# A new table of stage offsets for the planner that orders a fused attention and MLP kernel

## The chip, the core and the metric

The kernel runs on one core of a Trainium2 chip. The time is that of one execution on the device, in microseconds; of several runs the median is told. TensorE is called PE here, VectorE DVE, ScalarE ACT, GpSimd POOL and SyncE SP, as the profile has them.

## The reference

Local attention with block summaries, then a normalised MLP with a residual. Four batches, eight heads, 768 positions, head size 64; the model width is 512, the hidden width 2048. `v_sum` is the mean of v over blocks of 32, `k_sum` the maximum of k.

```python
scores_l = scale * np.matmul(q, k.transpose(0, 1, 3, 2))
mask_l = np.abs(pos[:, None] - pos[None, :]) < 16
scores_s = scale * np.einsum('bhsd,bhnd->bhsn', q, k_sum) + np.log(32)
scores_all = np.concatenate([np.where(mask_l, scores_l, -1e9), scores_s], axis=-1)
a = softmax(scores_all)
x = concat_heads(np.matmul(a, np.concatenate([v, v_sum], axis=2)))
xn = (x - mean(x)) / np.sqrt(var(x) + 1e-6) * g_ln
out = x + np.maximum(xn @ w_ch1, 0.0) @ w_ch2
```

## The kernel before

The rows of the 24 tiles of 128 positions (T, six to a batch) go through attention in 48 halves of four heads (t = 2T and 2T + 1). For one half, PE computes the scores `s` (`qk`, or `early_qk` for the first twelve halves, which are those of the first batch), DVE adds the mask and takes the maximum, ACT takes the exponential (`softmax`), the probabilities `p` are transposed to `pT`, and PE multiplies them with v into `o` (`pv`, `early_pv`). For the first batch the transposing is done on PE (tile `pp`) with a copy on ACT; later it is a transposing DMA that SP issues.

`ln(T)` normalises the 128 rows and writes them as two float16 halves, `x16`; `lnT(T)` has SP issue a DMA that transposes x16 into `xt`. One `xt` holds two tiles T, so that xt_2 takes x16_4 and x16_5. The MLP goes over twelve groups g of two tiles and eight steps j each. `g1(s)`, with s = 8g + j, makes the hidden tile `h` from xt and the first weights (24 matmuls; h16 to h23 are those of g = 2); ACT and DVE take it out of PSUM as two float16 parts. `g2(s)` adds its product with the second weights to the two accumulators `a` (`a0` those of g = 0); after j = 7 DVE adds the residual and SP stores. The very last accumulator of half a width is called `last`.

Weights arrive as pairs of 32-bit words (`raw`, 512 KB each). `merge_w` puts each of the 16 + 16 blocks together in three DVE steps (`m1_f`, `m2_f`), `gram` multiplies each block with itself on PE to bound its size, `scale_w1` and `scale_w2` make scales of that, and `split_w` splits each block into two float16 parts (`w_u` and `w`; the order's names for the latter are `w2_0` to `w2_15`), the first part on ACT, the second on DVE. `scale_w2` needs all 16 blocks of `gram` for the second weights, and every `a` needs `scale_w2`. For each batch after the first, maxima of k (`kmax`), sums of v (`vsum`) and bounds are taken from loads of `ks`, `vs` and `qa` that go through the buffers `bst` and `qs`; `batch_vput` has SP write vsum into the tiles of v with eight small DMAs.

No engine's order is written out. Every call is recorded as an operation of a stage, a call of a `step` function with its arguments. `issue` ranks each operation by the longest chain behind it, adds 16 times its stage's entry of the table `ORDER` (935 numbers), plans the program forward with `schedule`, where each engine takes its ready operation of the lowest rank, and then in turn backward and forward, `ROUNDS` times; of the forward plans the one with the earliest end is kept, and the operations are issued in the order of its planned starts:

```python
rank, best = [r + early[x.stage] for r, x in zip(rank, self.ops)], None
for _ in range(ROUNDS):
    start, end = self.schedule(rank, after, False)
    if best is None or max(end) < best[0]:
        best = (max(end), start, end)
    rank = [-x for x in self.schedule([-x for x in end], then, True)[1]]
```

On the chip each engine works through its own instructions strictly in that order, and SP issues all DMAs in its order. All recorded instructions carry the line that issues them, L333, so they are told apart by their tiles.

Of the kernel before, what the change touches and what calls it, by code (L numbers as in the profile page):

```python
# [49 lines left out]
PVS = 4  # L50

ORDER = (
    "Z{Yv`E;RrEJtzPGqUitsIN$&OEZ_hC@BaV)CiMUR_T~ToEd2lfG~@sOdfWg10~r7Sd;tIevEKjxD(L_J-sb=R?(_fuR@VRjF8Kfdfdl{m5aa*<"
# [4 lines left out]
    "7r&Mp7|%nkqm1y=w7$Ljz8L)!oUG3x*So(li~q4)p)Arb%pAUFU3HShobw(tM{ITHW?8}R@CPWJ!*B<TPD!pHyrlO6y7lI#EfSs4HT7cKw*w*&"
    "wHohSeRoCg2^au@&riz)yBHwgd$wlM$z2>1X0ef$6a(zpNrwG;pVeeeJO(f<Gc)(8Lq&>#Q+iopN>mgoQfFw+13?h60_G5-JmZyNvr-"
    "2wmre;@z=%mM%axD)^YN#y_k(iQ*!uq6NhOaK4>DF6Tel;r>aul@i3jQaoo84&;gFd+Z{nh*d0R~G;Pi~axqbqoLiMFs!>;`aal2=f2`@z($UD"  # L60
    "&+tF^9ld}{nY>eBnJQhJpBLv8x;Tm|NH;{Soi<`jPU>eN7VoSECT=lqy_*0KnVZ<{3`$eR4@Pl6Y~H6D&YVBRr3G;{KEhL0{s8~GbsQ7#UB6wT"
    "LJ(8&h`KQ_1*vf|Lgz%uNVLT<^TWydG`PRq0s;TsRsZ66x;v*(hUFr;Q#;t1IqvZ$OHfYzWM+E_4NP$j{pDwydD4my8ZwE&mI5(h6Dfr8Z7_-"
    "RNVjnYT*C>{uKZKrN;mNUIPFC4(0#<_SygcR}cUIa~S{t^!xw+l@b5|MPUE{Y3Tp|1Ni^{6aWAKgb@G$L#O}$U=jcTfG7X}&;0-Y>-"
    "Ycv!xjJl^eO-V?HvFB$pHWW^veJLfE)k-=I;OhDGdMs#Q*>RJ1GDFiBJFld?o+@#w7p%pfUge5+DEo%sv1BV>kc+N-"
    "Y2YKNA1|vl9RSE&u=k2LAv5Y&ZY_(kcJ|JU0LU2nGNEkKX_PWi<c*Tgw0c!^i*s^Z5V&@#z2mE9n3K<NyEvyHEfCRv7>Qhy?%u$PNGi8Z-"
    "a^=N13}=lTEt*a-jtPVoQ#1^NH~C>H<#p%nlCf*Sw;k~aVV3OE1&Yc>D?K_&nI#7zJIMic-"
    "5s2BhMZTbKIwg3PBG!g&+r49f93@iWufBpaeRuljLWG(;zN96ziJpcdzwe0`@x7h#x04M+eBme*ZP5uA>Vdnq;!w~=gwg3PCECB!j3jhEA+1vm"
    "Bch~>_9Q^<PO7Z{y91s8i5a|E^_b31WHvj+tD98W*5dZ)G#vK3v*9HIpr6m9WnEwC&#r^;PTM_^OOYi^x{Pq9;KOX=9VFLgFu=)T0ryKwPF!cZ"
    "bH_HG2UhDt=pBVrECdvQ*nacnFjPU>efyn>=h`Im&x(NUPw738NUakNCkQ4v_iv0ioaoqp^blU&_Y61WNZ!!P?;lcm^(dGaDy7&M8%o6|rd;tI"
    "e#k~Lj5y1cdgWmuDKG*;M$Ke0}@B#n;8r}c@5#9g)N!|bdInMw8lq~=NK?(o>_`d)DEE)g+M+X1^?cM+XQ``UluO9#aYOeqP&9VRg;Q{~vL+Jn"  # L70
    "il;!{be)RwU6|MjO{~7=Qhp_+u=Mew^V7LGOPU!#tx!wQ&e)|9a7>@t{BG~``dei^^bff?O#ialLtTF%q@74eRLgfGd3lsnVtQ`OVBo+Vw#1sG"
    "kR__1*W!C@y8Uz3UIRF3u-rfKI%E<r!kG22*r1}5<BP0L-"
    "h{XT@M%e%Va^C;{qV@m(Ow#}VbJqX=koo`r3*rC&GWq}i)Ykw1efa<Xq~QPmmJ9#@9mN0t9k2iYZr1<*{>1<PD3$;Jz~=w|yZQhBquu}iC@la0"
    "?8X28<=g-NgV+E60{#F0G!Fm(rP2TYM&|$jpbY>3;{gBwp11%1Llgi2BoY7sIqd)c9m@azOfUcd*DC-3MgIT)V-"
    "ElT+YbN$%N76tcoF~ryW;=<1Qq}QDG&evpBMlD1n&R;#K8amz{CIlK=c3qh6MlsG|&J4PaXgOIR*d#;wb<Cj1vF=W~%@H^Wp#hj`IKi6|(>T{o"
    "DWlHSz!dpY;F#P~HFkAQ}JwG6ettef$6an)v_!D&7D8k>UUUiu3>f$pioZiN^o`z!CrerMdtA-q!#Bi{=0Sin9Ozfa3rEw)g-47ux^-"
    "AoKtKCIA2b&C&n=^z{G#O8@`>e;)t<G~WOJeFp#l5CH%HXUqTp`U3y}!mR)Qj4=QJcm@CfLDc{Ma_;~CH~|0v4)Xv1jOYLVx6c3n^&0>HlnVd="
# [1038 lines left out]
```

## Time and profile before

| what | before |
| --- | --- |
| median of 3 runs | 643.07 us (639.03, 643.07, 643.48) |
| the profiled execution | 637.87 us |
| its span | 635.9 us |
| PE busy | 623.9 us (98%) |
| DVE busy | 440.5 us (69%) |
| ACT busy | 379.3 us (60%) |
| POOL busy | 198.8 us (31%) |
| DMA queue of the kernel | 93.34 MB, 56.8% of 16 engines' span |
| granted TensorE clock | 1.00 |

The span runs from the first instruction to the last; the profiled execution's own time has 1.97 us more around it. The end of a matmul is modelled, so a busy PE can still be waiting a little between two matmuls. In the time line a row gives the start, the time taken, the engine, what is written from what, how many, and in brackets how long the engine had been idle and what ended that. An SPq row is SP issuing a DMA, not the transfer. Buffer numbers are left out in the profile, so that h16 and h17 are both `h`.

### The profile page before, as it was taken

To read this page: it belongs to the slowest core of one execution; us is meant where nothing else is said; L and a number is where in the kernel's file an instruction comes from. 1 tells how busy PE (TensorE), PEld (TensorE's weight loads), DVE (VectorE), ACT (ScalarE), POOL (GpSimd) and SP (SyncE) were. 2 spreads that over 40 slices of the span, in tenths; PEclk is the share of its full clock that TensorE was granted. 3 is DMA by queue.
4 is the path that set the end of the run, shared out by engine and by line. 5 is a ranking of instruction groups with operands and counts; after the bars stand their busy time and mean duration, and the time that the engine had idled before them with its cause. 6 is when DMAs were issued, how large, how long until landed. Compare 5 with 4: busy or idle time off the path is not lost.

```text
span 635.9 us, 13651 instructions
## 1 busy us (share of the span) xinstructions
PE 623.9 (98%) x4795; PEld 442.5 (70%) x4795; DVE 440.5 (69%) x1158; ACT 379.3 (60%) x986; POOL 198.8 (31%) x406
## 2 busy tenths in 40 slices
...
GB/s 303 247 193 281 260 296 214 128 134 101 160 204 134 110 149 160 175 158 159 198 170 162 168 136 123 121 107 163 111 129 129 155 145 95 61 84 51 18 1 33
DMA packets 134837, 94.19 MB, mean 148 GB/s; under 512 B 88561, under 2 KB 119281, under 8 KB 134770
## 3 DMA queue, kind: packets, MB, share of 16 engines
q1 hardware_dynamic: 134770, 93.34, 56.8%
q8 instruction: 37, 0.61, 0.4%
q14 instruction: 30, 0.25, 0.1%
...
## 4 chain that ended last, share of the span: by engine, by line
PE 76%; DVE 10%; DMA 9%; ACT 3%; issue 1%; POOL 1%; SPq 0%; ACTq 0%; DVEq 0%; POOLq 0%
PE a L333 35%; PE h L333 31%; DVE m L333 4%; PE o L333 4%; PE s L333 4%; DMA raw<-in_w 3%; DMA spare_x<-in_qe 2%; DMA spare_x<-in_va 2%; DVE x L333 1%; DVE h_x L333 1%; DMA pT<-p 1%; ACT p L333 1%; DMA qs<-in_ks 1%; PE last L333 1%; DVE vsum L333 1%
## 5 line engine op out<-in xcount | busy, mean ns | idle before, releaser
L333 PE MATMUL h<-xt,w_u 128*128 128x256 f16 x2304 | 267.3, 273 | 4.3 <-issue 2.1
L333 PEld LDWEIGHTS <-w_u 128*128 128x128 f16 x2304 | 224.2, 98 | 37.2 <-issue 5.5
L333 PE MATMUL a<-w,h_x 128*128 128x512 f16 (+1 forms) x960 | 214.5, 374 | 0.1
L333 PEld LDWEIGHTS <-h_x 128*128 128x128 f16 x1008 | 97.2, 98 | 92.9 <-issue 0.3
L333 ACT ACTIVATE p<-p,mn,sv 128x184 f32<-128x184 f32 x144 | 76.1, 530 | 28.0 <-POOL mn L333 27.7
L333 DVE SCALAR_TENSOR_TENSOR h_x<-h,h_x 128x512 f16<-128x512 f32 x80 | 53.9, 684 | 48.2 <-ACT h_x L333 47.7
L333 POOL TENSOR_TENSOR p<-p,p 128x512 f16<-128x512 f32 x72 | 72.1, 1014 | 44.7 <-ACT p L333 42.8
L333 ACT ACTIVATE h_x<-h 128x512 f16<-128x512 f32 x80 | 45.9, 587 | 61.0 <-PE h L333 60.9
L333 DVE SCALAR_TENSOR_TENSOR kl<-ksg,sv,kh 128x368 f16<-128x368 f32 x72 | 49.4, 686 | 29.2 <-ACT kh L333 28.7
L333 ACT ACTIVATE kh<-ksg,sv 128x368 f16<-128x368 f32 x72 | 43.0, 597 | 36.8 <-POOL ksg L333 35.8
L333 DVE CUSTOM_DVE_ANT_0 p<-s,mask 128x184 f32<-128x184 f32 x144 | 44.7, 342 | 23.0 <-PE s L333 18.7
L333 POOL TENSOR_SCALAR mn<-mn,sv 128x2 f32<-128x2 f32 x72 | 28.5, 397 | 91.5 <-DVE mn L333 85.1
L333 ACT ACTIVATE bst<-bst 128x384 f32<-128x384 f32 (+2 forms) x55 | 32.3, 588 | 32.0 <-DVE vsum L333 11.8
L333 POOL COPY ksg<-ksum 128x48 f32<-128x48 f32 x72 | 20.2, 280 | 89.1 <-DMA ksg<-in_kt 75.5
L333 PE MATMUL a<-w,h_y 128*128 128x512 f16 x192 | 44.2, 379 | 0.0
L333 DVE SCALAR_TENSOR_TENSOR v<-vst,sv,v 128x256 f16<-128x256 f32 x72 | 41.2, 591 | 3.6 <-ACT v L333 3.0
L333 DVE SCALAR_TENSOR_TENSOR m<-raw,m 128x512 uint32<-128x512 uint32 x64 | 42.4, 681 | 0.1
L333 ACT ACTIVATE x<-xn,rs 128x512 f16<-128x512 f32 x24 | 17.2, 719 | 32.8 <-POOL rs L333 27.8
L333 ACT CAST p<-p 128x512 f16<-128x512 f32 x72 | 33.6, 505 | 4.8 <-DMA pT<-p 4.3
L333 POOL TENSOR_TENSOR x<-x,rc 128x256 f32<-128x256 f32 x36 | 24.7, 686 | 37.3 <-DVE x L333 37.2
L333 DVE TENSOR_REDUCE x<-o 128x256 f32<-128x512 f32 x36 | 24.6, 685 | 14.7 <-PE o L333 13.7
L333 ACT ACTIVATE qhl<-qs,sv 128x512 f16<-128x512 f32 x36 | 25.7, 713 | 11.8 <-PE s L333 10.1
...
## 6 DMA issues: line engine op xcount, KB each, us to landing
...
```

Source lines behind the costliest of these rows:

```text
L333: getattr(getattr(nc, self.ops[i].engine), op)(*a, **k)
```

## The change

The table `ORDER` has other numbers, and `ROUNDS` is 3 instead of 4. The new numbers were found by annealing on replays of the order with disturbed durations, the old ones by the planned end alone. Nothing else differs: the same operations, tiles and engines.

```diff
-ROUNDS = 4
+ROUNDS = 3
...
-    "Z{Yv`E;RrEJtzPGqUitsIN$&OEZ_hC@BaV)CiMUR_T~ToEd2lfG~@sOdfWg10~r7Sd;tIevEKjxD(L_J-sb=R?(_fuR@VRjF8Kfdfdl{m5aa*<"
...
+    "&E5b1{1yNJOBetEyyO4><lO)NOwa%S68``H_4oh(H1hxd?&AOdeZ>F&xzPXr^A7+3+28;Fg~R{<Dc}G9=D`2|d-"
...
```

What this does to the order is shown at three places. First SP's queue where the second half of xt_2 is transposed, at about 110 to 119 us of the profile before (`vsum1` are the sums of v for the second batch, `in_vb` and `in_kt` loads of v and k for later halves, `raw2_15` the last block of the second weights, `bst43` and `bst44` blocks of k for the third batch). Before:

```order
L333 DMA_TRANSPOSE xt_2_441<-x16_4_440 128x8x128
L333 DMA bst43_663<-in_ks 128x384
L333 DMA qs30_462<-in_qt 64x512
L333 DMA vst0_77<-vsum1_423 24x128 x4
L333 DMA vst1_78<-in_vb 32x256 x2
L333 DMA vst1_78<-vsum1_423 24x128 x3
L333 DMA raw2_15_357<-in_w2 128x1024
L333 DMA vst1_78<-vsum1_423 24x128
L333 DMA_TRANSPOSE xt_2_441<-x16_5_446 128x8x128
```

And now:

```order
L333 DMA_TRANSPOSE xt_2_441<-x16_4_440 128x8x128
L333 DMA bst26_430<-in_vs 96x512
L333 DMA raw2_15_357<-in_w2 128x1024
L333 DMA qs30_462<-in_qt 64x512
L333 DMA vst1_78<-in_vb 32x256 x2
L333 DMA qs30_462<-in_qt 64x512
L333 DMA bst43_663<-in_ks 128x384
L333 DMA vst0_77<-vsum1_423 24x128 x4
L333 DMA vst1_78<-vsum1_423 24x128 x4
L333 DMA bst44_664<-in_ks 128x384
L333 DMA_TRANSPOSE xt_2_441<-x16_5_446 128x8x128
```

The load of raw2_15 and the two loads of `in_vb` for vst1 now stand right behind the first half of xt_2, ahead of the writes of vsum and no longer among them; the eight writes of vsum and one block of k still go ahead of the second half.

Then ACT, where the hidden tiles are evacuated at about 119 to 130 us (`h14_x5<-h15` is the evacuation of h15). Its order mirrors that of PE's groups. Before:

```order
L333 ACTIVATE v16_1_377<-vst1_78,sv1_435 128x8x64
L333 ACTIVATE h12_x4_401<-h13_402 128x512
L333 ACTIVATE bst44_664,vabs2_662<-bst44_664 128x384
L333 ACTIVATE h16_x6_448<-h16_447 128x512
L333 ACTIVATE kh12_1_471<-ksg12_1_470,sv1_435 128x368
L333 ACTIVATE qhl13_480<-qs31_479,sv1_435 128x512
L333 ACTIVATE p_87,sum12_469<-p_87,mn12_468,sv1_435 128x184 x2
L333 ACTIVATE h14_x5_404<-h15_405 128x512
```

And now:

```order
L333 ACTIVATE h14_x5_404<-h14_403 128x512
L333 ACTIVATE bst44_664,vabs2_662<-bst44_664 128x384
L333 ACTIVATE kh12_1_471<-ksg12_1_470,sv1_435 128x368
L333 ACTIVATE h14_x5_404<-h15_405 128x512
L333 ACTIVATE bst45_666,vabs2_662<-bst45_666 128x384
L333 ACTIVATE h16_x6_448<-h16_447 128x512
```

The group h15, which reads xt_1, stood behind h16, the first that reads xt_2; now it stands ahead of it, and h13 is further up.

Last PE's beginning (`warm` are transposes of the identity, `gain` spreads g_ln over the partitions, `v0` sums v of the first batch by blocks, `s0` are the first scores). Before:

```order
L333 MATMUL warm_102<-ident_76 128x128 x36
L333 MATMUL s0_0_107<-ident_76 128x128
L333 MATMUL s0_0_107<-spare_x6_100,spare_x0_93 128x184
L333 MATMUL s0_1_108<-spare_x6_100,spare_x0_93 128x184
L333 MATMUL s0_0_107<-spare_x6_100,spare_x0_93 128x192
L333 MATMUL s0_1_108<-spare_x6_100,spare_x0_93 128x192
L333 MATMUL v0_106<-spare_x1_96,blk_86 120x512
L333 MATMUL gain_104<-xn1_103,ones1_79 128x512
```

And now:

```order
L333 MATMUL warm_102<-ident_76 128x128 x36
L333 MATMUL gain_104<-xn1_103,ones1_79 128x512
L333 MATMUL v0_106<-spare_x1_96,blk_86 120x512
L333 MATMUL s0_0_107<-ident_76 128x128
L333 MATMUL s0_0_107<-spare_x6_100,spare_x0_93 128x184
L333 MATMUL s0_1_108<-spare_x6_100,spare_x0_93 128x184
L333 MATMUL s0_0_107<-spare_x6_100,spare_x0_93 128x192
L333 MATMUL s0_1_108<-spare_x6_100,spare_x0_93 128x192
```

`gain` and the first matmul of v0 have moved ahead of the first scores.

More of the change, by code (lines that the diff above doesn't have):

```diff
@@ L58 @@
[L58 to L77, printed above, removed]
@@ L102 @@
-    "3=4d&vL);hq2g|4sk^P$~cbH30wsixmI>;@toL8|?r8R|Eh6G1&kAT@(NS0|Ed5G}!<DZ1VsA9x?y`*xLX9m-zqx"
+    "&E5b1{1yNJOBetEyyO4><lO)NOwa%S68``H_4oh(H1hxd?&AOdeZ>F&xzPXr^A7+3+28;Fg~R{<Dc}G9=D`2|d-"
+    "DJP;miO31>XPv^#}j}TG#*o79s!u;TQk_j0FGyR5btq0RR90z7qfd;`RUk#S#DjydD4meG32pZ#@72B#r<73H$&5W&r>IX|@0VIQ{?s*X;lQV;"
+    "=wjsn-AhVeS9_kemPi$GZRjfuH~Xr{e$rw7~!W7qI{Tz@-2Ghv5JJh|K^0hspo{-"
+    ">CopOP&A!Kb!ymq`d$CaK!)rVb%Zt!;Am_X`uiA_?7?v7_a~TQH=lpDY^gu+oJ#f=KufyR;>U3w%`B%#hU;B{I381&$s{o2dDr4S<wIgVUGX*_"
+    "1ORatKk3tc*p<$_xu0<+Uo!R*RTKo?uGyV@YDbQPOty}rN00FOz8jrNbdjtmGJ-nGvNRKX~6&g!}<UJ$*uqY9OnQ3Ql0<*W5ECac#{ABVaEUet"
@@ new lines @@
+    "r!3R*Z%+iQFj0ULHqyzR>}YW7~}u{?Hd39q1ONZh6(@xye<F$yxsr*^xgme_6Gm}V(kC_Nx%R9lGFeH`n~`EwGsdTeaZj-"
+    "+Wr6k+#dh{Ne%!2;5h&QSpxt7^ArF8c^CiyRQUh@G#~%~8rT2-"
+    "fcgLbZjk@~nezYt^8o+=vitx4|Kk7uH0S^SwyOXCHLL&sj==x_3kCoHrvU%}Egt{?H|ziZbNB!MfDixxY7qbclllMuj~4&{S6l!9J@)_qJ>CER"
+    "mFoZh3*P_#2KxX1k?jBfkS72D5Fr2nfh7O{EfD|!b`Ssn$@2gI-QEBHmhJ!lpyB`js@DJiKjHuX!|nh7Jk<aHo(up0R{a0}vh@G|C(-}^>f-"
+    "<ZywU&v!U_NYK=c3qb|e4*7cT$+tS$fm(#`+>+t~mA=GFiIrO5yPo)!QAA|C(%DF*-"
+    "mCI|okJoEqmzs~>vBJ2PE5(@wTz4QP7p#T5?ZPWk%H2?qqNYwxTv=9IQqWk~<SlR#ox&;6L$oT*N4cPzxu@nFRMJ50MjPd{f#~J_to%#R&@G<}"
@@ new lines @@
+    "ZN9_Oqf8hWBiWvX^`P={h#25eoj^_XW?dAXfF%tj)m=OQ~(E|Vgoh$$VO<Di|L(TvHS@-|{<N*Kx{uclM_mBVolp+8Clve-%f!hE7T=)O~OZ@-"
+    ";+&cgO(gy$lW%U35FU$Y`Y#{&ujL-"
+    "l7LmU7A3grL)?MMIsC_4ZEoiqRdALRf4`9=T$#{d8SpGW`zQV{?E^Ev<kVITkivjhMDxeNdRA>;r50wn+dSv~*&d0zkkCnf*@f7$>4Whwvw&Gr"
+    "BPqWb^;^y~lsMfm^!kJkVHq38eqluQ5sa}@vpBN+eyVL<=@vpoO+pC14Kdlmoy3JU-LChh<KM;ibDZ$AJ49vJ`tttS8gvONF*J|_SG>N@}cjT8"
+    "U?5?ufQ<|6<AJs$u7knI2ehUowQ(GUOtEf@d*N+JLNCky}pycPfe#5e!|0^<Mw7ySSKZ~*`SS>ylzkskm6+5`XqlkNZiINtyN5)=Rcm;3+!O8N"
@@ new lines @@
+    "i)hz$S$Q~Lk^<+}g>yyE}=3;h58X%+wgGU5OK6dwQphV=jc$Eg4R;rajn;2Zz|u>Al3954U?<lX=OSP1|Cwf_JAL;e5%sp0?sKo<Z29t;2gUiJ"
+    "U~Y#aapEB^ogZN2~hH{AdK8~OkL9+3b4kiY-`ZtDO49LWFwji>+rPTl|i2#){%U#0*5Z36%RiSqydVc-"
+    "A%;MM>CwEqA9;xPaK^T+@H9`XPG!Vv%fzXt#S3K0MR{<Hu8wekP|!N&jp?a=@KFzWyRJ{SN1mCgVEFzx^US<C<bth@jJ6dV8mFem^39Jl}fu<Q"
+    "T-;`IOj8Pfm%I>-P2fBXOc7s~(t1iSzLO#}b{vBCfU82kVKsn`Gi{<Z)ACjbBc#jOAT4FUiF8>9dKQ^5cK3-"
+    "AB`2m1g2q?`Z$+PnY%Y}5b$Xr%xDPPPC4c}V~OxxN4YOv?ZN6&wHn=P&>O#|HoaAte9+3n~Br&e8w>cRT<9c@_Ww*yI2IQr-XmGQj`;PvrmqQV"
@@ new lines @@
+    ";+D@}B?yE8hSAchvv?;_Uzbh1UQ7gUA2>%MJhl#q9t8Xz~C5K+6CB74-"
+    "lA0NDTkB<cVEe&zrF{G|W?wZH%WtMUK;&#nLehy(xts_Fm#d*uKBQak_vb-n-po$vqu!~6gLGY<d&yZ8V9THgQvj_Uva_YMF6_xk_;q0;~V78w"
+    "8lFaZDn`s)Axv6BD)2SNY<4JZHr3i$v3bo~GSPeT9zOcekCEi(WBDFFZg3;O^6OBVnD8X*7xTJQh=nW_K(7_<NX+4BGYwGjXSd)5E{h9dv~dk6"
+    "pkniBv3u^0dVN{IjeLg4@Z<kSEE&949d7Tf>-ujK##KIQ-"
+    "a(A)q2Lm~hGAMOADe)#|Y&)fh1L*4)Xw9Wtja0vha+Y<l)qTB!fr}h8;Gok<g*v|j|?$H1Lf1LmS(BJ?6NeTb}{MG;egz^9XB>VsWtg-"
+    "+9H0b~T3GDy>E*}5@x~KpDq#XbNEbagQ!K?rOUo8Ltt-1gI{}liLDfIvU;<Eq$J(U0dB-Q`_V7UMPpRoV`i^Ko_BlrLRR~!HUFs1+hh}r-"
@@ new lines @@
+    "D#5Vu{AM*eIwe$b~OgR7mbO-<d>mmRE4+;PP+baM7_1ypeIT-"
+    ")|ye|L%!_5ExuT=m5@Cg6_#xno_4G91Mn9TqGYZw3kkL&;cHp~D2aPj~D1Frx7;3EJ4Z^!@tBk2GCBG3Q-"
+    "?!y27B{Bd2j{X1thdKZN4b%VsbPoUkj!pmo+D!leTTTD~!VCZa03`qbgaZHo+B*OMdrklVraS-u?f?J)F8Tle$t(Z>Iz9jZ3-"
+    "$m1^dtZPbus_|6UG1k`|1Dxd5-"
+    "`8QqTYY{j&f6=lK8seT)D9$H4#p9hLw8!H56<4BG$yBI*DCGnW7V_74C6z2pD?snP%cHthfZK(GJ*=JEgkOrHP$g1P_yY?uH40ptJwOPc@xSFQ"
+    "j5GW-Ak<|qIF`nCW6K;i%Y!m$7UAprmY#kT+d`<(y(D)s;W8OQ(s$NB&N@9zKq0384T3Zwu34Eq27{7(P?DP#Zu0~G)OH&Orq@b~}!dA9%mL;("
```

45 lines of the change are left out of this document (17 added, 28 removed).

## The prediction

> **What bounds the kernel now.** I read the page first, then the busy time by stage, then TensorE's waits, and then the time lines around the longest of them.
>
> ```profile
> span 635.9 us, 13651 instructions
> PE 623.9 (98%) x4795; PEld 442.5 (70%) x4795; DVE 440.5 (69%) x1158; ACT 379.3 (60%) x986; POOL 198.8 (31%) x406
> PE 76%; DVE 10%; DMA 9%; ACT 3%; issue 1%; POOL 1%; SPq 0%; ACTq 0%; DVEq 0%; POOLq 0%
> 157.36 1.31 PE h L333 x12
> 154.21 1.29 PE a L333 x6
> ```
>
> TensorE (PE) is busy 623.9 of 635.9 us and holds 76% of the chain that ended last. The last two rows, pieces of that chain in order of time, show what a busy PE delivers: twelve matmuls of an h tile take 1.31 us and six of an `a` tile 1.29 us. The reorder issues the same 2304 h matmuls, 1104 full `a` matmuls and 96 half ones: 2304 x 1.31 / 12 = 252 us, 1104 x 1.29 / 6 = 237 us and 96 x 1.31 / 12 = 10 us. These 499 us don't change with the order. What an order can win is idle time, and this view by stage has it (columns: busy us and count of PE, PEld, DVE, ACT, POOL, then granted clock, DMA share, GB/s):
>
> ```profile
> 0.00:45.00 45.00, 42.34 (x280) 30.76 (x281) 33.29 (x123) 33.31 (x110) 12.58 (x69) 1.00 0.80 250
> 45.00:110.00 65.00, 64.14 (x528) 50.79 (x526) 62.19 (x171) 54.43 (x167) 13.68 (x26) 1.00 0.85 262
> 110.00:145.00 35.00, 31.15 (x306) 27.58 (x305) 29.73 (x85) 20.41 (x50) 9.39 (x17) 1.00 0.52 135
> 145.00:170.00 25.00, 25.00 (x172) 15.01 (x170) 23.36 (x48) 22.47 (x52) 8.48 (x15) 1.00 0.46 115
> 170.00:270.00 100.00, 99.94 (x684) 61.44 (x683) 68.11 (x174) 59.15 (x152) 34.89 (x63) 1.00 0.61 157
> 270.00:626.00 356.00, 354.67 (x2778) 251.28 (x2776) 222.88 (x557) 189.57 (x460) 119.76 (x217) 1.00 0.51 119
> 626.00:635.94 9.94, 6.63 (x61) 5.69 (x59) 0.97 (x2) 0.00 (x0) 0.00 (x0) 1.00 0.08 26
> ```
>
> PE idles 2.7, 0.9, 3.9, 0.0, 0.1, 1.3 and 3.3 us in these seven stages, 12.1 us in all. Of the first stage 1.8 us lie ahead of the first matmul, and the last 3.3 us are the last evacuation and the store behind it. Both orders begin with the warm tile and end with 48 matmuls of the tile `last`, so these 5.1 us stay. About 7 us are in an order's reach, 3.9 of them between 110 and 145 us. From 145 us on PE idles 1.4 us before the store: a new order can hardly win there, only lose.
>
> ```profile
> PE h L333 <- issue: 2.1, 1, 2.1
> PE h L333 <- DVE h_x L333: 1.6, 3, 0.7
> PE o L333 <- ACT pT L333: 1.3, 3, 0.5
> PE s L333 <- DVE kl L333: 0.7, 1, 0.7
> PE h L333 <- DVE scales L333: 0.5, 1, 0.5
> ```
>
> One wait of 2.1 us, put down to no releaser, is the largest. Its place and what stands behind it (PE, then DVE, then SP's queue):
>
> ```profile
> 117.50 2.78 PE L333 MATMUL h<-xt,w_u 128*128 128x256 f16 x24 [0.71 <-DVE h_x L333]
> 120.12 0.62 PE L333 MATMUL gram<-m 128*128 128x128 bf16 x8
> 122.86 2.78 PE L333 MATMUL h<-xt,w_u 128*128 128x256 f16 x24 [2.11 <-issue]
> 125.47 0.24 PE L333 MATMUL s<-kh,qhl 128*128 128x184 f16 x1
> 114.79 0.75 DVE L333 SCALAR_TENSOR_TENSOR x<-xn,rs,x 128x512 f16<-128x512 f32 x1 [1.16 <-ACT x L333]
> 110.40 3.27 SPq L333 DMA_DIRECT2D vst<-vsum  x4
> 117.62 0.73 SPq L333 DMA_DIRECT2D vst<-vsum  x1
> 118.45 1.28 SPq L333 DMA_TRANSPOSE xt<-x  x1
> ```
>
> The group that waits is h16, the first that reads xt_2. DVE finished the second half of its source (x16_5) at 115.54, but SP issued the transposing DMA at 118.45, behind the writes of vsum and a weight load, and PE could go on 4.4 us after that issue. So I take "issue" here as this DMA.
>
> **The change part by part.** Each engine issues the same instructions; only places move.
>
> *h16, the one term that I can size.* By the order, 24 matmuls of h15 and twelve gram matmuls of m2_9 to m2_11 now stand ahead of h16 instead of behind it: 2 x 1.31 + 12 x 0.0575 = 3.3 us (0.0575 is 0.92 / 16, first row here).
>
> ```profile
> 30.76 0.92 PE gram L333 x16
> L333 DVE SCALAR_TENSOR_TENSOR m<-raw,m 128x512 uint32<-128x512 uint32 x64 | 42.4, 681 | 0.1
> 111.50 0.85 POOL rs L333
> 112.42 1.59 POOL rs L333
> ```
>
> Without its wait PE would have been at h16 at 122.86 - 2.11 = 120.75; now at about 124.05. Against this, x16_5 comes later. On DVE nine instructions more stand ahead of it: three second and third merge steps (0.6 us each; the row has 42.4 us for 64, with its overlaps), one first step (0.5), the evacuation of h11 (0.6), a kmax (0.5) and three small ones, 3.7 us together. Of this the 1.16 us for which DVE had waited just there come off, so x16_5 starts near 114.79 - 1.16 + 3.7 = 117.3. By its other chain, the last matmuls of o11 come 2.6 us later on PE (36 gram matmuls more, 2.6 us; one half h group exchanged for another), and then POOL's rs (2.4 us) and ACT stand between: 118 at most. It ends 0.7 us later. On SP a weight load and two loads of vb have left the places ahead of this transpose; eight writes of vsum (3.27 / 4 = 0.8 us each) and one block of in_ks stay. vsum itself is ready 4.8 us of DVE work later, eight steps of 0.6 us again, so the eight writes end near 118.5. The transpose is issued at 118.5 to 119.5 and lands 4.4 us later at 122.9 to 123.9; PE is there at 124.05 and doesn't wait. Bounds: -2.1 us, or 0 if vsum's writes slip 2 us more; below -2.1 nothing, as this wait has no more. I take -2.1, though the landing may be ahead by as little as 0.1 us.
>
> *The start.* `gain` and one matmul of v0 now go ahead of the first scores s0. They take 1.05 us each, from start to start:
>
> ```profile
> 8.95 1.12 PE L333 MATMUL v<-spare_x,blk 128*120 128x512 f32 x2
> 10.00 1.12 PE L333 MATMUL gain<-xn,ones 1*128 1x512 f32 x2
> 11.05 1.12 PE L333 MATMUL v<-spare_x,blk 128*120 128x512 f32 x2
> ```
>
> so the first softmax, on DVE and ACT, starts 2.1 us later, while o3 and s5 stand behind as much PE work as before. Bounds: +2.1 us if nothing takes this up, and -0.7 at best, the waits for pp and pT that lie there. What takes it up is room: ACT and DVE are each 33 of 45 us busy in this stage, so both wait 11.7 us in it. The loads hold it no longer than that: s0's q now stands behind two more loads of v (256 KB each) and the block table (72 KB), which at the stage's 250 GB/s is 2.4 us, about what s0 itself has moved. I take 0, nearer to the room than to the price.
>
> *45 to 110 us.* DVE is 62.2 of 65 us busy, DMA 85%; the merges of the weights change places among themselves. PE has h work that fills; it idles 0.9 us. Bounds: -0.9, or +2 us for a merge that once waits a whole 512 KB load (2.0 us at 262 GB/s); taken 0.
>
> *scale_w2 and the first `a` tile.* The matmul that ends gram2 comes 5.7 us of PE work later, `a0` 5.9 us later, and all of h16 to h23 now stand ahead of `a0`. The margin there before:
>
> ```profile
> 138.51 0.28 PE L333 MATMUL gram<-scales,ones 128*128 128x1 f32 x2
> 141.13 4.10 PE L333 MATMUL h<-xt,w_u 128*128 128x256 f16 x36 [0.45 <-DVE scales L333]
> 145.64 1.67 PE L333 MATMUL a<-w,h_y 128*128 128x512 f16 x7
> 145.24 0.56 PE o L333 x12
> 148.39 0.32 PE s L333 x4
> 141.99 1.32 ACT L333 ACTIVATE w<-m,scales 128x512 f16<-128x512 f32 x2
> 142.73 1.42 DVE L333 SCALAR_TENSOR_TENSOR w<-m,scales,w 128x512 f16<-128x512 f32 x2 [0.55 <-ACT w L333]
> 164.05 0.74 DVE L333 SCALAR_TENSOR_TENSOR w<-m,scales,w 128x512 f16<-128x512 f32 x1
> ```
>
> w2's first two tiles end at 144.15, some 1.5 us ahead of `a0`; the sixteenth ends at 164.8. From the gram matmul to `a0` PE had 145.64 - 138.51 - 0.45 = 6.7 us of work; now h22, h23, o12 and s14 stand there, 4 x 1.31 + 0.56 + 2 x 0.32 + 0.4 = 6.8. After it `a0` runs with no h group between: where two half groups of h (2.6 us) stood ahead of its fifth pair of w2, there is now one group of scores more. So w2 is used up to 3 us sooner after `a0`'s start, and I estimate the margins at 0.5 to 1.5 us. Price: -0.5 (the wait for scales) to +4.4 (the third rival below); taken 0.
>
> *From 170 us.* Counted in PE work at 1.31 and 1.29 us per group, the shortest distances are like before: from scores to o 12.2 us in both, from an h group to the reuse of its PSUM buffer 1.6 us now and 1.9 before, from h to `a` 1.6 and 1.95; the reuse of an `a` buffer after 1.3 us occurs once, before twice. A miss costs what the waits show, up to 0.7 us. Bounds -1.4 to +2.5; taken 0.
>
> The sum against the profiled execution (637.87 us with 1.97 around its span of 635.9): 637.87 - 2.1 = 635.8 us. Extremes: with all 7 us of waits gone 631; with every upper bound 637.87 + 2.1 + 2 + 4.4 + 2.5 = 648.9.
>
> **To the median.** The three timed runs are 639.03, 643.07 and 643.48: the profiled execution lies 1.2 us under the lowest and 5.2 under the median. PE's products are the same each time, so at least the 4.0 us between lowest and median are something that varies, and no row says what. If it is fixed for this comparison, the median goes to 643.07 - 2.1 = 641.0; if it is waits that a different order doesn't meet, to 639.03 - 2.1 = 636.9. I take the middle, 639.0.
>
> [...] PE came out of its 2.11 us wait at full speed: 24 h matmuls in 125.47 - 122.86 = 2.61 us, granted clock 1.00. [...]
>
> **The rivals.**
> - *The order also takes away what varied* (20%): the median reaches 636.9 or less, down to 634, which is 635.8 without the waits of 1.8 us for h_x and pT that the list has beside h16's, rounded. For it: 3.7 us of the waits listed are for h_x and this one DMA, which a late load makes longer. Against it: no row shows them longer.
> - *Nothing gained* (22%): xt_2 moves with h16, since o11 and x16_5 moved nearly as far (2.6 and 3.7 us against 3.3), or as much is lost after 145 us. Time 643, between 641.5 and 645.
> - *The w2 splits fall behind* (13%), the one that ends slower. The sixteen splits took 164.8 - 142.0 = 22.8 us, 2.85 a pair, with ACT 22.5 and DVE 23.4 of 25 us busy; PE now takes a pair each 2 x 1.29 = 2.6 us with no h group to fill. Over eight pairs that is 8 x 0.25 = 2.0 us; if four evacuations of h that it had between still wait on ACT or DVE (0.6 us each, as above), 4.4. It decides when a split comes over 1.5 us later relative to the gram matmul. With the h16 wait gone 643 to 645.4, with it 645 to 647.5; I price it 645. [...]
> - *Anything over 1% slower* (5% within the last) needs this and the start's 2.1 us together.
>
> **How the numbers follow.** Forecast 45%: 639.0, its own range 636.9 to 641. The range reaches down to 634.5, half-way into the first rival, and up to 645.5, over the second and most of the third. A measurement here tells about 1% from no change: under 636.6 is faster, over 649.5 slower. Faster: the first rival and a little of the forecast, 0.24. Slower: 0.05. The same: 0.71.
>
> **What would show it.** Right: h16's group without a wait of over 0.5 us, the transpose of x16_5 landing before it; the stage from 110 to 145 us with under 2 us idle; PE's idle time in all 9 to 11 us. Wrong: PE waiting for w within the first eight groups of `a0`, for pT before 30 us by over 1 us, or idle over 3 us after 170 us. If PE's idle time falls and the median doesn't, my bridge from profile to median was wrong.

## The result and the profile after

The changed kernel took 634.9 us in the median against 643.3 for the kernel before; the ratio is 0.988 (95% interval 0.984 to 0.992). A second measurement gave 0.989 (0.987 to 0.991). The forecast was 639.0 in a range of 634.5 to 645.5: the time is inside, near its lower end, and it is the first rival's time ("the order also takes away what varied", down to 634). The profiled execution took 633.33 us. Executions much longer than the rest (one of the changed kernel at 651.6 us and a mean clock of 0.949, one of before at 1320.5, and some of other kernels above 900) count in these two medians, which are 634.6 and 643.1 without them, and are left out of the ratios and of everything below.

The head of the page, and the chain's shares by engine:

```profile
span 631.5 us, 13647 instructions
PE 622.1 (99%) x4795; PEld 441.9 (70%) x4795; DVE 433.4 (69%) x1158; ACT 378.5 (60%) x986; POOL 199.5 (32%) x406
PE 83%; DVE 9%; DMA 5%; ACT 2%; issue 0%; SPq 0%; POOL 0%; ACTq 0%; POOLq 0%
```

TensorE (PE) idles 631.5 - 622.1 = 9.4 us, 2.6 less than before, and its busy time fell too, from 623.9 to 622.1, with the same 4795 matmuls. Busy and idle time by stage (same columns as in the prediction):

```profile
0.00:45.00 45.00, 42.04 (x284) 30.75 (x285) 33.14 (x124) 33.38 (x114) 13.08 (x69) 1.00 0.84 254
45.00:110.00 65.00, 63.70 (x539) 50.77 (x538) 61.94 (x172) 52.47 (x159) 11.44 (x24) 1.00 0.87 263
110.00:145.00 35.00, 33.94 (x332) 30.32 (x330) 29.63 (x86) 23.32 (x59) 12.13 (x23) 1.00 0.50 132
170.00:270.00 100.00, 100.00 (x692) 62.16 (x690) 68.90 (x184) 59.71 (x154) 35.79 (x68) 1.00 0.65 160
270.00:621.00 351.00, 350.24 (x2747) 248.25 (x2745) 217.49 (x546) 186.06 (x451) 118.67 (x208) 1.00 0.49 117
```

From 110 to 145 us PE idles 1.1 us where it idled 3.9. PE's waits (us in all, times, longest):

```profile
PE warm L333 <- POOL ident masks.py:199: 1.6, 1, 1.6
PE o L333 <- ACT pT L333: 1.2, 2, 0.8
PE h L333 <- DVE h_y L333: 0.8, 1, 0.8
PE h L333 <- DVE h_x L333: 0.7, 1, 0.7
```

The 2.1 us put down to "issue" are gone, and behind the start nothing waits over 0.8 us. The place of that wait, on PE, SP's queue and DVE:

```profile
116.69 5.42 PE L333 MATMUL h<-xt,w_u 128*128 128x256 f16 x48
121.94 0.62 PE L333 MATMUL gram<-m 128*128 128x128 bf16 x8
123.23 2.78 PE L333 MATMUL h<-xt,w_u 128*128 128x256 f16 x24 [0.67 <-DVE h_x L333]
112.11 6.22 SPq L333 DMA_DIRECT2D vst<-vsum  x8
118.44 0.45 SPq L333 DMA_DIRECT2D bst<-in_ks  x1
118.99 1.27 SPq L333 DMA_TRANSPOSE xt<-x  x1
121.12 0.55 DVE L333 TENSOR_REDUCE kmax<-bst 128x12 f32<-128x384 f32 x1 [2.21 <-DMA bst<-in_ks]
122.49 0.69 DVE L333 SCALAR_TENSOR_TENSOR h_x<-h,h_x 128x512 f16<-128x512 f32 x1
```

The transpose of x16_5 is issued at 118.99, as forecast (118.5 to 119.5). The trace has its completion at 122.62, and PE was ready for h16 at 123.23 - 0.67 = 122.56: it came just in time. In the kernel before it had completed at 122.76, with h16 starting at 122.86, so "issue" was this DMA, as the prediction took it. h16, the group at 123.23, now waits for something that the prediction had not looked at: DVE's evacuation of an h tile at 122.49, which stands on DVE behind a `kmax` that waited 2.21 us for a block of in_ks. SP had issued that block behind the same eight writes of vsum. The kernel before had this stall as well, unseen beside h16's own wait:

```profile
123.27 0.55 DVE L333 TENSOR_REDUCE kmax<-bst 128x12 f32<-128x384 f32 x1 [2.05 <-DMA bst<-in_ks]
123.86 0.68 DVE L333 SCALAR_TENSOR_TENSOR h_x<-h,h_x 128x512 f16<-128x512 f32 x1
```

Of the change's two edits only the table acts: with the new table, four rounds instead of three lead the planner to the same order on every engine.

### The profile page after: what moved, and what is told of

It reads as the page before. It is cut to its first block, busy times and chain, and to the rows that moved or that the text cites. A ratio compares the mean times of both kernels' runs of the same rounds, so it can differ in the third digit from the quotient of the medians.

```text
span 631.5 us, 13647 instructions
## 1 busy us (share of the span) xinstructions
PE 622.1 (99%) x4795; PEld 441.9 (70%) x4795; DVE 433.4 (69%) x1158; ACT 378.5 (60%) x986; POOL 199.5 (32%) x406
## 3 DMA queue, kind: packets, MB, share of 16 engines
HBM read 66.27 MB, written 6.29 MB: 115 GB/s over the span
## 4 chain that ended last, share of the span: by engine, by line
PE 83%; DVE 9%; DMA 5%; ACT 2%; issue 0%; SPq 0%; POOL 0%; ACTq 0%; POOLq 0%
PE a L333 39%; PE h L333 32%; PE s L333 5%; PE o L333 4%; DVE m L333 4%; PE v L333 1%; DMA bst<-in_ks 1%; DMA qs<-in_vs 1%; DMA blk<-in_blocks 1%; PE last L333 1%; DMA raw<-in_w 1%; DVE h_x L333 1%; DVE vsum L333 1%; DMA ksg<-in_kt 1%; DMA qs<-in_qa 1%; PE pp L333 1%
## 5 line engine op out<-in xcount | busy, mean ns | idle before, releaser
L333 POOL TENSOR_TENSOR p<-p,p 128x512 f16<-128x512 f32 x72 | 70.7, 993 | 39.3 <-ACT p L333 31.0
L333 DVE SCALAR_TENSOR_TENSOR kl<-ksg,sv,kh 128x368 f16<-128x368 f32 x72 | 46.5, 645 | 23.5 <-ACT kh L333 22.8
L333 POOL TENSOR_SCALAR mn<-mn,sv 128x2 f32<-128x2 f32 x72 | 25.7, 356 | 103.1 <-DVE mn L333 100.3
L333 POOL TENSOR_TENSOR x<-x,rc 128x256 f32<-128x256 f32 x36 | 26.4, 734 | 46.5 <-DVE x L333 46.3
L333 DVE SCALAR_TENSOR_TENSOR x<-a,scales,x 128x512 f32<-128x512 f32 (+1 forms) x24 | 17.7, 736 | 24.0 <-PE a L333 23.7
```

Of the source, the lines that this page charges most:

```text
L333: getattr(getattr(nc, self.ops[i].engine), op)(*a, **k)
```

## The experiments

**Repeats: what varies.** The question left by the prediction was what lies between the profiled execution of before and its median. Both kernels were run again, unchanged.

> The kernel before, unchanged, profiled a second time. Its times lay between 639.0 and 644.7 us, and its profiled execution at 637.87, so no row has yet shown where the 4 to 6 us between lie. Theory A (one place: a late load or a wait like h16's 2.1 us that is sometimes longer): the new profile, if its time is 641 or more, has one or two waits on TensorE that are longer than before, idle time in all 15 us or more instead of 12.1, and the rest of the stages alike within 0.5 us. Theory B (spread over the whole span: many small gaps that the busy time hides): idle time within 1 us of 12.1 and a busy time that is 3 us or more above 623.9. Ratio to the kernel before 1.000, interval within 0.993 to 1.007.

> The kernel before, unchanged, one more profile: about half of its executions have a mean clock of 0.997 or less and are 2.7 us longer. Theory 'window': if the profile is one of them, the granted clock falls to half for about 3.4 us within 5 us behind h16's wait, which is then 2 us or more; the matmuls there take twice their time, 1.7 us or so in all. Rival: the lower clock stands elsewhere, by another wait. If the profile is at 1.000 it says nothing on this; idle time between 110 and 145 us then 3.8 to 4.8 us as in the two others.

> The changed kernel, unchanged, profiled a second time, as the yardstick for the edits of it. Its first five executions had spans of 631.5 to 633.9 us, all at a mean clock of 1.000. Theory 'less varies' (no wait near 2 us stands in the new order, so no execution loses a clock window): spans of 631.5 to 635, none or one of twelve at 0.997 or less, ratio 0.986 to 0.990; between 110 and 145 us TensorE idles 1 to 2 us. Rival 'the first executions were lucky': the second profile has a wait of 1.5 us or more between 90 and 130 us, a quarter or more of the executions are at 0.997 or less, ratio 0.991 to 0.995.

Measured: before against itself 1.0001 (0.9974 to 1.0027); its two further profiles have spans of 637.7 and 637.2 us, both at a mean clock of 1.000. The changed kernel again: 0.9894 and six spans of 631.7 to 633.5 us, that of the second profile 632.5, as the theory "less varies" had it. The stage from 110 to 145 us in the two further profiles of before, then in the second of the changed kernel:

```profile
110.00:145.00 35.00, 30.41 (x305) 26.96 (x304) 29.55 (x84) 19.02 (x45) 9.29 (x17) 1.00 0.53 132
...
110.00:145.00 35.00, 31.43 (x310) 27.82 (x308) 29.88 (x85) 20.27 (x50) 9.10 (x17) 1.00 0.55 137
...
110.00:145.00 35.00, 33.35 (x324) 29.78 (x322) 29.29 (x84) 23.86 (x60) 11.23 (x22) 1.00 0.51 135
```

Idle there: 3.9, 4.6 and 3.6 us before, 1.1 and 1.7 after. h16's wait was 2.1, 2.7 and 2.1 us in before; in the second profile of the changed kernel h16 waits 1.24 us for h_x.

Each execution also lists its mean granted clock, and there the kernels differ most. Of 98 executions of before on three chips, 48 had a mean clock of 0.999 or 1.000 and a mean span of 637.6 us (standard deviation 1.3), and 50 had 0.995 to 0.997 and 640.4 us (1.7). A mean of 0.997 is what 3.4 us at half clock in 638 give (3.4 / 2 / 638 = 0.0027); such a stretch stands in the profile of the changed kernel with the writes spread, shown below (0.51 over 3.4 us), and by this count it costs 3.4 / 2 = 1.7 us, an estimate. 45 of the 50 had 0.996 or 0.997; five had 0.995, as two such stretches give. The rest of the 2.8 us between the two groups is not taken apart. All 11 executions of the changed kernel had 1.000 and a mean span of 632.7 us (0.7). Neither theory named for the first repeat covers this: its profile, at 639.9 us, was too quick for A (641 or more), and its busy time was 0.7 us above 623.9, where B had 3 or more. The profiles at full clock differ by small waits at several places, and half of the executions had a mean clock of 0.995 to 0.997 besides. No execution of before at the lower clock fell to a profile, so where its clock fell was not seen.

**h16 alone.** The order of before, with the PE work of the forecast's term put ahead of h16 by hand:

```diff
+        best = list(old)
+        at = min(old[i] for i, x in enumerate(self.ops) if x.engine == "tensor" and x.stage == self.stages["g1", (16,)])
+        first = [("gram", (9, 2)), ("gram", (10, 2)), ("gram", (11, 2)), ("g1", (15,)), ("g1", (16,)), ("qk", (12, 0)), ...]
+        for n in first:
+            ...
+                    best[i] = at
+                    at += x.busy
+        for i in range(len(best)):
+            best[i] = max([best[i], *(best[j] + 1 for j in self.ops[i].after)])
```

> The order of before with one edit: the 24 matmuls of h15 and the gram matmuls of m2_9 to m2_11 go ahead of h16, as in the changed kernel, and everything else keeps its place (three instructions of DVE and one of ACT change places behind it). The forecast's term alone: h16's wait of 2.1 us goes, TensorE idles 1.0 to 2.0 us between 110 and 145 us instead of 3.85, a profiled execution of 635.8 us, a ratio of 0.996 to 0.998. Rival 'h16's wait was also what varied': the ratio is that of the changed kernel, 0.986 to 0.990. Rival 'nothing gained': the wait turns up again within 20 us, ratio 1.000.

Measured: 1.0023 (0.9994 to 1.0051), and a span of 640.1 us in the profile. PE, then DVE:

```profile
125.78 2.78 PE L399 MATMUL h<-xt,w_u 128*128 128x256 f16 x24 [1.23 <-DVE h_x L399]
130.91 1.47 PE L399 MATMUL h<-xt,w_u 128*128 128x256 f16 x12 [1.35 <-DVE sv L399]
124.46 0.55 DVE L399 TENSOR_REDUCE kmax<-bst 128x12 f32<-128x384 f32 x1 [2.73 <-DMA bst<-in_ks]
125.05 0.68 DVE L399 SCALAR_TENSOR_TENSOR h_x<-h,h_x 128x512 f16<-128x512 f32 x1
130.17 0.69 DVE L399 SCALAR_TENSOR_TENSOR h_x<-h,h_x 128x512 f16<-128x512 f32 x1 [2.58 <-ACT h_x L399]
```

The wait for the DMA is gone, and five others have its place (1.23, 1.35, 1.19, 0.48 and 0.65 us, for h_x and sv): the stage idles 6.2 us (28.80 of 35 busy), more than before. While PE waited for the transpose, DVE had waited for in_ks; once PE no longer waits, it meets the h_x that stand behind `kmax`. The rival "nothing gained" holds for this edit. So 3.3 us of PE work ahead of h16 do not bring the 2.1 us alone; the new order also has the evacuation of h13 ahead of `kmax`, and the 48 h matmuls of h14 and h15 (5.2 us) run beside its stall. That these two make the difference was not tested by themselves.

**SP's queue alone.** Eight writes of vsum hold SP for 6.22 us, 0.78 each, with the transpose and the in_ks block behind them. In four kernels the last four writes go further back, and the order of the rest is kept (`best` is the plan of before or of the changed kernel):

```diff
+        sp = lambda name, *a: [i for i, x in enumerate(self.ops) if x.engine == "sync" and x.stage == self.stages[name, a]]
+        last = max(best[i] for i in sp("lnT", 5) + sp("batch_k", 2, 0)[1:2])   # "first": behind the transpose and in_ks
+        last = max(best[i] for i in sp("lnT", 5) + sp("load_q", 13))           # "spread": behind the loads that follow, too
+        for n, i in enumerate(sp("batch_vput", 1, 1)):
+            best[i] = last + 1 + n
```

> The order of before with one edit on SP's queue: the last four writes of vsum go behind the transpose of x16_5 and the block of in_ks, all other engines keep their order. Theory Q (both stalls there have one cause: SP issues a write of vsum in 0.78 us, and the transpose that h16 needs and the block of in_ks on which DVE's kmax waits 2.0 to 2.7 us stand behind eight of them): the transpose issues 2 us earlier, h16's wait goes without a new one, DVE's wait at kmax falls under 0.7 us, TensorE idles 1.5 to 2.0 us between 110 and 145 us instead of 3.9 to 4.6; executions at a mean clock of 0.997 or less fall from about half to under one in five; ratio 0.992 to 0.996. Rival 'the stage is bound by DVE's evacuations in any case': h_x waits take the place as in the kernel with h16 moved, ratio 0.998 to 1.003.

> The same edit on the changed kernel: the last four of the eight writes of vsum go behind the transpose of x16_5. Theory Q: DVE's wait of 2.2 us at kmax and the 0.67 us that h16 waits for h_x behind it go; profiled execution 0.5 to 1 us under the changed kernel's, ratio to before 0.986 to 0.990. Rival: the transpose waits for x16_5 with the block of in_ks behind it, no gain, or the late writes of vsum hold the first v; ratio 0.989 to 0.995.

> The same on the order of before: four writes of vsum behind the transpose, the next loads of in_ks, in_kt, in_qt, and ACT's second v behind an h_x and a bst. Theory Q (the writes alone hold this place): h16's wait of 2.1 to 2.7 us goes and none over 1 us comes between 110 and 145 us, TensorE idles 1.5 to 2.2 us there; executions at 0.997 or less under one in five; ratio 0.992 to 0.996. Rival 'one edit only shifts the wait' (as with h16 moved, and with the writes moved less far): a wait of 1 us or more for h_x, kmax or v stands there, ratio 0.998 to 1.003.

> The changed kernel with the last four writes of vsum moved further on SP: behind the transpose of x16_5, the next loads of in_kt and in_ks and two of in_qt, with the load of in_vb that follows them; ACT's second v, which reads them, goes two instructions later. In the kernel where they were moved only behind the transpose, ACT waited 3.3 us for them at that v, with an h_x behind it, and h16 2.15 us for this h_x. Theory Q: no consumer waits over 1 us there; h16's wait is under 0.4 us, DVE's at kmax under 0.7 us; ratio 0 to 0.2% under that of the changed kernel repeated. Rival: SP is short of time whatever stands behind (8 writes by 0.78 us), a load behind them becomes the late one; ratio 0.2 to 0.7% above it.

Measured: on the order of before 1.0017 (0.9990 to 1.0044) for the first place and 1.0025 (1.0000 to 1.0050) for the second; on the changed kernel 0.9951 (0.9926 to 0.9976) and 0.9952 (0.9932 to 0.9972), both 0.6% slower than the changed kernel itself at 0.9894. All four were expected to gain by the theory on the queue; none did. The first one has no profile that can be read; 2 of its 11 executions had a mean clock of 0.997 or less. In the other three the same thing stands. On the changed kernel with the writes behind the transpose (DVE), and on the order of before with them spread (ACT, DVE):

```profile
121.59 0.55 DVE L396 TENSOR_REDUCE kmax<-bst 128x12 f32<-128x384 f32 x1 [0.35 <-DMA bst<-in_ks]
126.30 0.69 DVE L396 SCALAR_TENSOR_TENSOR h_x<-h,h_x 128x512 f16<-128x512 f32 x1 [3.37 <-ACT h_x L396]
...
127.18 0.72 ACT L396 ACTIVATE v<-vst,sv 128x512 f16<-128x512 f32 x1 [6.29 <-DMA vst<-vsum]
127.81 0.58 ACT L396 ACTIVATE h_x<-h 128x512 f16<-128x512 f32 x1
128.42 0.69 DVE L396 SCALAR_TENSOR_TENSOR h_x<-h,h_x 128x512 f16<-128x512 f32 x1 [6.26 <-ACT h_x L396]
```

`kmax` is rid of its stall, 0.35 us instead of 2.21, just as the theory had it. But ACT reads the late writes in its second `v` and waits for them (6.29 us in the second case; 3.30 in the first), and behind that `v` stands the h_x that DVE and then PE need: h16 waits 2.15 us in the first case, an h group 3.10 us in the second. The queues of PE, DVE, ACT and SP are bound together in this stage; a step moved on one of them alone moved the wait to the next.

**Front or steady part.** Two kernels join the two plans at a cut where their sets of finished work differ least (9 instructions at 165 us):

```diff
+        best = [t if t < 165e3 else 1e6 + u for t, u in zip(new, old)]   # new_to_165
+        best = [u if u < 164e3 else 1e6 + t for t, u in zip(new, old)]   # new_from_165
```

> The changed kernel's order up to 165 us of the plan on all engines (scores, weights' merging, gram matmuls, the first a tile), and the order of before from there on. The sets of instructions ahead of the cut differ by 9 of some 3,200. Theory 'front': the 8 us that the change gained in the median lie in the part where loads fill the DMA queues; ratio 0.985 to 0.990, profiled execution 633 to 635 us. Theory 'steady part': the gain lies behind the cut; ratio 0.996 to 0.998 (h16's 2.1 us alone), profiled 635 to 636.

> The other half: the order of before up to 164 us, the changed kernel's order behind. Theory 'front': ratio 0.998 to 1.001, h16's wait of 2 us is there as before. Theory 'steady part': ratio 0.988 to 0.993, with TensorE's busy time 1.5 us or more under 623.9 and its idle time behind 170 us under 1 us.

Measured: 0.9961 (0.9938 to 0.9984) and 1.0079 (1.0050 to 1.0109). The first ratio is the one expected for a gain in the steady part, but neither kernel answers cleanly, since the joint itself costs. Behind it, new front with old rest, then old front with new rest:

```profile
170.00:270.00 100.00, 97.08 (x663) 59.33 (x662) 67.56 (x174) 56.71 (x146) 34.46 (x61) 1.00 0.59 151
...
180.50 0.31 PE L390 MATMUL s<-kh,qhl 128*128 128x184 f16 x1 [3.44 <-ACT kh L390]
181.54 5.09 PE L390 MATMUL a<-w,h_x 128*128 128x512 f16 x12
180.50:186.50 6.00, 5.67 (x17) 2.31 (x17) 5.52 (x19) 3.35 (x10) 2.46 (x6) 0.52 0.67 206
```

The first idles 2.9 us between 170 and 270 us, where both full orders idle under 0.1; without these its mean span of 637.1 would be 634.2, and its stage from 110 to 145 us idles 2.2 us. That puts most of the gain ahead of 165 us, by subtraction only. In the second, a wait of 3.44 us at the joint is followed by half clock (0.52 over 6 us): twelve `a` matmuls take 5.09 us, against 1.29 for six in the prediction's row. All 10 of its executions had a mean clock of 0.997 or less.

**Room for other durations.** In both kernels, each `bn_stats` of a norm is issued twice, which neither plan expects:

```diff
             for op, a, k in self.ops[i].calls:
-                getattr(getattr(nc, self.ops[i].engine), op)(*a, **k)
+                for _ in range(2 if op == "bn_stats" else 1):
+                    getattr(getattr(nc, self.ops[i].engine), op)(*a, **k)
```

> The order of before, with every bn_stats of the norms issued twice: 24 more instructions of DVE of 0.6 us, 14.4 us in all, for which neither order was planned. Theory 'room' (the new table's order keeps more room for durations that come out otherwise): before loses 3 to 7 us here, ratio 1.005 to 1.011. Rival 'one place' (the change gained because it avoids one stall, and has no more room elsewhere): before and the changed kernel lose the same within 1 us.

> The changed kernel's order with the same 24 instructions more. Theory 'room': it loses 0.5 to 3 us against the changed kernel's 632.8 us of mean span, less than half of what before loses; ratio to before 0.988 to 0.993. Rival 'one place': it loses what before loses within 1 us, ratio 0.993 to 0.999.

Measured: 1.0116 (1.0089 to 1.0144) and 0.9964 (0.9943 to 0.9985). In mean spans before goes from 639.4 on the same chip to 645.8, a loss of 6.4 us, and the changed kernel from 632.7, not measured on that chip, to 636.7, a loss of 4.0. That is more than half of 6.4, so "room" had the size too small, and 2.4 us apart, so "one place" falls. The part from 145 to 621 us, without the extra work and with it, before first, then the changed kernel:

```profile
145.00:621.00 476.00, 474.61 (x3590) 323.83 (x3588) 313.61 (x778) 271.18 (x662) 163.13 (x294) 1.00 0.53 127
145.00:621.00 476.00, 469.81 (x3548) 319.60 (x3549) 325.78 (x808) 274.21 (x673) 162.20 (x296) 1.00 0.56 129
...
145.00:621.00 476.00, 475.24 (x3583) 323.81 (x3581) 307.67 (x776) 269.29 (x657) 162.87 (x291) 1.00 0.53 128
145.00:621.00 476.00, 474.03 (x3587) 323.60 (x3585) 321.37 (x804) 271.54 (x664) 165.11 (x294) 1.00 0.54 127
```

PE idles 6.2 us there in before, which without the extra work idles 1.4; in the changed kernel 2.0 against 0.8. In the steady part, then, the new order does keep more room: it loses 1.2 us where the old one loses 4.8. Ahead of 145 us both lose 2.2 to 2.4 us (idle 7.4 to 9.7 us in before, 5.3 to 7.5 in the changed kernel, where a wait of 2.1 us for `vm` and one of 1.3 for h_x are new). It is one profile of each.

**Waits and the clock.** All runs together, the longest wait of PE behind the start in each kernel's profile against the executions with a mean clock of 0.997 or less:

| order | longest wait, us | at 0.997 or less |
|---|---|---|
| changed kernel (two profiles) | 0.8, 1.2 | 0 of 11 |
| h16 alone | 1.35 | 1 of 11 |
| new to 165 us | 1.5 | 0 of 12 |
| changed, writes spread | 2.1 | 3 of 12 |
| changed, more DVE | 2.1 | 2 of 12 |
| changed, writes behind the transpose | 2.15 | 4 of 12 |
| before (three profiles) | 2.1, 2.7, 2.1 | 50 of 98 |
| before, more DVE | 2.3 | 2 of 6 |
| before, writes spread | 3.1 | 7 of 12 |
| new from 165 us | 3.4 | 10 of 10 |

With longest waits up to 1.5 us 1 of 34 executions was at 0.997 or less, from 2.1 to 3.1 us 68 of 152, at 3.4 us all 10. One profile shows half clock behind a wait as long as h16's, in the changed kernel with the writes spread (PE; then the stages, with the granted clock third from the end):

```profile
132.75 4.26 PE L396 MATMUL h<-xt,w_u 128*128 128x256 f16 x24 [2.07 <-DVE h_x L396]
137.17 2.82 PE L396 MATMUL h<-xt,w_u 128*128 128x256 f16 x24 [0.16 <-DVE h_x L396]
130.40:133.80 3.40, 1.33 (x15) 1.05 (x13) 1.74 (x5) 2.18 (x5) 0.00 (x0) 1.00 0.41 119
133.80:137.20 3.40, 3.24 (x17) 2.16 (x16) 2.17 (x8) 2.94 (x9) 1.58 (x7) 0.51 0.51 132
```

After 2.07 us of waiting the granted clock is 0.51 for 3.4 us, and 24 matmuls take 4.26 us instead of 2.78. PE idled 2.07 of the 3.4 us ahead of that, no more. In before's first profile a wait of 2.11 us was followed by full clock (1.00, and 24 matmuls in 2.78 us).

The length alone does not tell the two cases apart; in these profiles the place does. Each trace lists when its granted clock changed, and the stretches between were whole multiples of 3.413 us (3.41 us at half clock in the changed kernel with the writes spread, 6.83 in the new order from 165 us; at full clock 631.47 us or 185 of them in before, 628.05 or 184 in the changed kernel). With the time counted on in steps of that length from a profile's own first change, PE idled 1.80 us or less (the width less its busy time) in every step between the start and the last matmul of the thirteen readable profiles, but for two: 2.07 us right ahead of the loss above, and 2.37 us right ahead of the one at the joint. Longer waits that were followed by full clock lay across two steps: of before's 2.11 us 1.55 lay in one and 0.57 in the next. The two with a loss, then the fullest without one (the changed kernel with the writes behind the transpose; before with the writes spread, which has two; before; before again):

```profile
130.46:133.87 3.41, 1.34 (x15) 1.04 (x13) 1.81 (x5) 2.12 (x5) 0.00 (x0) 1.00 0.42 123
176.02:179.43 3.41, 1.04 (x5) 0.39 (x4) 0.00 (x0) 0.58 (x3) 0.85 (x2) 1.00 0.24 77
...
123.27:126.69 3.42, 1.62 (x19) 1.39 (x18) 0.39 (x1) 1.63 (x4) 0.03 (x1) 1.00 0.27 72
124.24:127.65 3.41, 1.82 (x17) 1.48 (x16) 0.00 (x0) 0.47 (x1) 0.00 (x0) 1.00 0.06 13
127.65:131.06 3.41, 1.90 (x19) 1.74 (x19) 2.61 (x9) 1.91 (x5) 0.63 (x1) 1.00 0.17 26
118.88:122.29 3.41, 1.86 (x21) 1.55 (x19) 2.31 (x4) 1.75 (x4) 0.00 (x0) 1.00 1.00 233
123.31:126.73 3.42, 1.99 (x19) 1.81 (x20) 1.58 (x4) 1.82 (x4) 0.80 (x2) 1.00 0.72 179
```

So in these profiles 1.80 us idle or less in one step was followed by full clock, and 2.07 and 2.37 us by half; what makes the clock fall is not shown. How often a wait goes with a lower clock the table alone tells: 50 of 98 executions of before, whose longest waits are 2.1 to 2.7 us, 11 of 42 of the other kernels with waits of 2.1 to 2.3 us, 7 of 12 with 3.1, and 1 of 22 of the changed kernel and h16 alone together, with 0.8 to 1.35.

That before's own lost clock comes from h16's wait is thus a reading of this table and these steps, and no trace shows it. With h16 moved the wait went, and 1 of 11 executions was left at the lower clock; that kernel has other waits instead (its executions at full clock have a mean span of 640.1 us, before's 637.6), so that its time did not fall.

## Why the prediction was right and where it was not

The mean spans give the account: 639.0 us (98 executions) to 632.7 (11), 6.3 us less. Three parts add up to it. The executions at the lower clock make 50/98 x (640.4 - 637.6) = 1.4 us. PE's idle time in the profiles at full clock fell from 12.0, 13.1 and 12.8 to 9.4 and 9.6, 3.1 us in the mean. PE's busy time fell from 623.9, 624.6 and 624.4 to 622.1 and 622.9, 1.8 us. The last two rest on three profiles and two. No run isolates them, so the account is a balance, and the cause of most of the gain is argued from it.

- **h16, -2.1: the size about right, the reason incomplete, and luck in it.** The stage from 110 to 145 us idled 4.0 us in the mean and now 1.35, 2.65 less. The places on SP came out as worked out, and x16_5 was 1.2 us ahead of its estimate (116.14 for 117.3). PE, though, was at h16 at 122.56 and not at 124.05, and by the forecast's 4.4 us the transpose would have landed at 123.4, 0.8 us too late. It landed 3.6 us after its issue (3.2 in the second profile; 4.3 to 4.6 in before's three), so two misses cancelled. But the step "24 matmuls and twelve gram matmuls stand ahead, so PE does not wait" is refuted by the kernel that does only this: it gained nothing. DVE's wait for in_ks, in the same 2 us and from the same queue, was the term left out. With it, h16 still waits 0.67 and 1.24 us, above the 0.5 set as the mark.
- **The start, 45 to 110 us, scale_w2 and a0: taken 0, and 0.** Idle time ahead of 45 us is 2.7 us in all three profiles of before and 3.0 and 2.5 after; between 45 and 110 us 0.9, 1.5 and 1.5 against 1.3 and 1.1. PE waits for no w in the first groups of `a0`. The price of the start (2.1 us) was taken up.
- **From 170 us, taken 0: 0.5 gained.** 1.4, 1.1 and 1.8 us of idle time up to 621 us became 0.8 and 1.1. "A new order can hardly win there, only lose" was right in size; the forecast counted distances, and the runs with more work on DVE show that they hold more than before's.
- **Busy time, left out of the sum: -1.8, of which 0.7 is no merit of the order.** "These 499 us don't change with the order" holds for the h and `a` matmuls, but the busy time also holds gaps between matmuls of different kinds, and the start. Counted from start to start over all 4795 matmuls, with waits taken off, what lies above the median distance of each shape is 9.6, 10.3 and 10.1 us in before's profiles and 7.8 and 8.6 after: 0.7 less in the `warm` tile, 0.3 between 45 and 110 us, 0.5 between 110 and 145, 0.3 behind. The `warm` tile's 36 matmuls open both orders. They took less where full clock was granted earlier, from 4.4 and 5.3 us on in the changed kernel's two profiles (5.46 and 5.91 us) and from 6.3, 7.3 and 6.2 us in before's (6.32, 6.81 and 6.29 us). That moment goes with the execution: in the four other kernels that open with the new order it lay between 5.4 and 7.6 us. Of the gain, 0.44 us came back in the first profile as a wait for `blk`. The other 1.1 us is a count from the traces; no run took it apart. First profiles, before and after:

```profile
1.76 6.32 PE L333 MATMUL warm<-ident 128*128 128x128 f32 x36 [1.76 <-POOL ident masks.py:199]
1.65 5.46 PE L333 MATMUL warm<-ident 128*128 128x128 f32 x36 [1.65 <-POOL ident masks.py:199]
```
- **The bridge to the median: the step that failed.** The forecast put the excess of the median, 5.2 us above the profile, half-way between fixed and avoidable. The repeats show what it was: the profiled execution on record was a quick one (635.9 against 637.6 in the mean at full clock), and half of the executions are 2.8 us longer at a lower clock. In the changed kernel the first is smaller, its profiled execution being 1.2 us under its mean, and the second is gone. So the rival given 20% came true, for a cause that it did not name, and the range held the time because it had been drawn half-way into that rival. The rival's own sum was off: its list has 1.6 us for h_x and 1.3 for pT, 2.9 and not 1.8, so that its lower end would be 632.9 instead of 634.
- **The clock.** The prediction's row had PE come out of a 2.11 us wait at full speed, and it set no price on the clock behind such a wait. The row of 24 matmuls behind 2.07 us of waiting differs: a clock of 0.51 for 3.4 us, 4.26 us instead of 2.78. All of the 2.07 us lay in one step of 3.41 us, of before's 2.11 us no more than 1.55. Why half clock follows in some executions and not in others, no run shows; what they show is the lower clock in 50 of 98 executions of before and in none of 11 of the changed kernel.
- **Chances.** Faster by over 1% had 0.24, and that is what came (the first interval reaches 0.992); 0.71 stood on the same. Of the signs for being right, the idle times came (1.1 and 1.7 us in the stage, 9.4 and 9.6 in all); h16 without a wait over 0.5 us did not. The rival "nothing gained" describes the edit of h16 alone, and "the w2 splits fall behind" did not occur.
